# Attention inputs loaded straight into the layout of their transposes, and weight conversions cut into three parts per attention step

## The chip, the cores and the metric

The kernel runs on one core of a Trainium2 chip. The metric is the device time of one execution in microseconds (us). In the profile PE is the matrix engine, PEld its weight loads, DVE the vector engine, ACT the scalar engine, POOL the GpSimd engine and SP the engine that issues most of the transfers. L12 is line 12 of the kernel file.

## The reference

Three computations follow each other; all of the output depends on all three.

```python
# attention: B=4, H=12 heads, S=448, D=64
scores = scale * (q @ k^T) - log(S)
attn_out = sigmoid(scores) @ v                  # -> x, 1792 tokens x 768
# mixture of experts, one expert of 8 per token, F=1024
e = argmax(x @ w_gate);  gate = softmax(x @ w_gate)[e];  eom = sigmoid(x @ w_output_gate)
x[token] = gate * eom[e] * (relu(x @ w1[e]) @ w2[e])
# last stage, d_ff = 2048
h = x @ w_in;  g = h * cos(h);  out = g @ w_out
```

The two matrices of the last stage, `w_in` and `w_out`, arrive as 64-bit floats, and q, k, v and the other weights as 32-bit floats.

## The kernel before

Every matrix product is made of several PE passes over a high and a low part of each operand (`kh`, `kl`; `gh`, `gl`; and so on). ACT rounds a value to its high part, and DVE subtracts that from the value to get the low part.

**Attention** runs from about 0 to 255 us, in 24 steps, one for each batch and pair of heads. A step has two halves, c = 0 and c = 2. In program order, a half does the scores of two of four groups of 112 keys (`sc`, L309; ACT turns them into `aT` with the sigmoid, L312), the transposes of the next step's operands on PE, and the product of the step before with v (`av`, L316). The transposes of c = 0 are those of q (`pq`, L294, then two DVE operations `T`, L302) and of the first head of k (`pk`, L282, then ACT `kh` L286 and DVE `kl` L288); c = 2 has the second head of k, and the transposes of the finished x (`px`, `xr`). The end of a step copies `av` out (`xT`, L326).

The transposes read q as 112 rows of (4 key groups, 2 heads, 64) and k as 112 rows of (4 key groups, the same head twice, 64). Memory holds each head apart. So `load` fetches q, k and v in the order of memory, one transfer each of 1 KB runs, three steps ahead, and `relay` copies two steps ahead: q on POOL (L271), the first head of k on POOL and the second on DVE (L276), the latter two doubling the head.

**Conversions.** The 64-bit weights are turned into two 32-bit parts on chip, in 48 pieces of 128x512 elements, and written back to memory (`wi_d`, `wo_d`) for the last stage. A piece is loaded (`craw`, two buffers); ACT makes `ctu` (L151); DVE makes `cta`, `ctf`, `cta`, `ctf` (L152 to L155); that is the first part of the generator `conv`. The second part is DVE `cta` (L157), ACT `chi` (L159) and three POOL operations (L160, L161, L163), the last of which writes `clo`. `ctu`, `cta` and `ctf` have one buffer each, so a piece's first part waits for the POOL operations of the piece before. An attention step ends with the first part of a piece (`conv_step(False)`), and c = 0 of the next step ends with its second part (`conv_end`). `conv_step` also issues, on SP, the stores of the piece before and the load of the next. Attention does 23 pieces this way; the expert slots bring the count to `CONV_EARLY` = 40; the rest are done in the last stage.

**Experts** run from about 255 to 690 us in slots of 128 tokens, with 17 pieces between them.

**Last stage**, from about 690 us, has 64 units u: 4 blocks of tokens times 16 chunks of d_ff. Iteration u of its loop issues a piece's first part while pieces are left, then `product(u + 1)`, `angle(u + 2)` (five DVE operations, L1152 to L1156, that reduce h for the cosine) and `down(u)` (the product with w_out). `product` multiplies h with its cosine, `r` on DVE (L1167), finishes the pending piece with `conv_end`, and then makes `gh` on ACT (L1171) and `gl` on DVE (L1172). The call `load_w(u + 5)`, ahead of `product`, finishes pieces whole until those are done that its chunk needs. The pieces are done during u = 2 to 9.

The order on each engine is the order in which the program issues; no planner moves it.

Of the kernel before, what the change touches and what calls it, by code (L numbers as in the profile page):

```python
# [9 lines left out]
F32 = mybir.dt.float32  # L10
# [11 lines left out]

GATE_STEPS = 7
NEST = 18
CONV_EARLY = 40
PAUSE = "pause"
NRING = 6
ROUTE_AT = [(0, "relu"), (0, 9), (0, 13), (0, 15), (1, 0), (1, 3), (1, "relu"), (1, 9), (1, 14)]
# [25 lines left out]
def tile_attn_moe_cos(ctx: ExitStack, tc: tile.TileContext, q, k, v, wg, wog, w1, w2, w_in, w_out, out):  # L54
    nc = tc.nc
    B, H, S, D = q.shape
# [4 lines left out]
    CP = 112  # L61
    NC = S // CP
    NPAIR = H // 2
# [40 lines left out]
    first = cst.tile([1, 1], I32, name="first")  # L104
# [24 lines left out]
    def conv_load(i):  # L129
        if i >= len(conv_list):  # L130
            return
        which, h, r = conv_list[i]
        raw = craw[i % 2]
        if which == "i":
            src = w_in[r * P : (r + 1) * P, h * CW : (h + 1) * CW].bitcast(U32)
            nc.sync.dma_start(raw.rearrange("p f t -> p (f t)"), src)
        else:
            src = wo_in[h][:, :, r * CO : (r + 1) * CO].bitcast(U32)
            nc.sync.dma_start(raw.rearrange("p (two f) t -> p two (f t)", two=2), src)

    def conv(i):
        if i >= len(conv_list):
            return
        which, h, r = conv_list[i]
        raw = craw[i % 2]
        low, high = raw[:, :, 0], raw[:, :, 1]
        ta = cta
        tf = conv_p.tile([P, CW], U32, tag="ctf", name="ctf")
        tu = conv_p.tile([P, CW], F32, tag="ctu", name="ctu")
        f = tf.bitcast(F32)  # L150
        nc.scalar.activation(tu, low, AF.Copy, scale=2.0**-52)  # L151
        nc.vector.tensor_scalar(ta, high, 3, 0x3FFFFFF8, op0=ALU.logical_shift_left, op1=ALU.bitwise_and)  # L152
        nc.vector.scalar_tensor_tensor(tf, high, 0xC0000000, ta, op0=ALU.bitwise_and, op1=ALU.bitwise_or)  # L153
        nc.vector.tensor_scalar(ta, high, 0x7FFFFFFF, None, op0=ALU.bitwise_and)
        nc.vector.scalar_tensor_tensor(f, ta.bitcast(F32), LEAST, f, op0=ALU.is_ge, op1=ALU.mult)  # L155
        yield
        nc.vector.tensor_scalar(ta, tf, 0xFF800000, None, op0=ALU.bitwise_and)  # L157
        hi = conv_p.tile([P, CW], F32R, tag="chi", name="chi", bufs=2)
        nc.scalar.activation(hi, f, AF.Copy)  # L159
        nc.gpsimd.tensor_tensor(tu, tu, ta.bitcast(F32), op=ALU.mult)  # L160
        nc.gpsimd.tensor_tensor(f, f, hi.bitcast(F32), op=ALU.subtract)  # L161
        lo = conv_p.tile([P, CW], F32R, tag="clo", name="clo", bufs=2)
        nc.gpsimd.tensor_tensor(lo, tu, f, op=ALU.add)  # L163
        conv_out.append((which, h, r, (hi.bitcast(F32), lo.bitcast(F32))))

    def conv_store():
        while conv_out:
            which, h, r, parts_ = conv_out.pop()
            for t, f in enumerate(parts_):
                if which == "i":  # L170
                    c0 = h * CW // P
                    nc.sync.dma_start(
                        wi_d[c0 : c0 + CW // P, :, t, r, :].rearrange("c p f -> p c f"),
                        f.rearrange("p (c f) -> p c f", f=P),
                    )
                else:
                    nc.sync.dma_start(
                        wo_to[h, t][:, :, r * CO : (r + 1) * CO], f.rearrange("p (two f) -> p two f", two=2)
                    )
# [3 lines left out]
    def conv_step(whole=True):  # L183
        conv_end()
        conv_store()
        conv_load(conv_at[0] + 1)
        conv_rest.append(conv(conv_at[0]))
        next(conv_rest[0], None)
        conv_at[0] += 1
        if whole:  # L190
            conv_end()

    conv_rest = []

    def conv_end():
        while conv_rest:
            next(conv_rest.pop(), None)


    pre = pre_st.enter_context(tc.tile_pool(name="pre", bufs=1, side="right"))  # L200
# [46 lines left out]
    with ExitStack() as st:  # L247
        io = st.enter_context(tc.tile_pool(name="io", bufs=3))
# [3 lines left out]
        ps_sc = ps_s.enter_context(tc.tile_pool(name="ps_sc", bufs=2, side="right", space=PSUM))  # L252
        ps_av = st.enter_context(tc.tile_pool(name="ps_av", bufs=1, space=PSUM))

        srcs = (("q", q), ("k", k), ("v", v))
        vt = [io.tile([CP, 2, NC, D], F32, name=f"v{i}", bufs=1) for i in range(5)]

        def load(b, hp):
            r = {}
            for nm, src in srcs:  # L260
                t = vt[(b * NPAIR + hp) % 5] if nm == "v" else io.tile([CP, 2, NC, D], F32, tag=nm, name=nm, bufs=2)
                nc.sync.dma_start(
                    t.rearrange("p h c d -> p h (c d)"),
                    src[b, 2 * hp : 2 * hp + 2].rearrange("h (p c) d -> p h (c d)", c=NC),
                )
                r[nm] = t
            return r

        def relay(t, first=nc.gpsimd):
            qp = io.tile([CP, NC, 2, D], F32, tag="qp", name="qp", bufs=2)  # L270
            first.tensor_copy(qp.rearrange("p c h d -> p h c d"), t["q"])  # L271
            t["q"] = qp
            for j in range(2):
                kd = io.tile([CP, NC, 2, D], F32, tag=f"kd{j}", name=f"kd{j}", bufs=2)
                eng = nc.vector if j else first
                eng.tensor_copy(kd, t["k"][:, j].unsqueeze(2).to_broadcast([CP, NC, 2, D]))  # L276
                t[f"k{j}"] = kd

        def prep_k(t, j, kk):
            pt = ps_tr.tile([P, 512], F32, tag="tr", name="pk")  # L280
# [212 lines left out]
        items = [(b, hp) for b in range(B) for hp in range(NPAIR)]  # L493
        n = len(items)
        L = {i: load(*items[i]) for i in range(3)}


        relay(L[0], nc.vector)
        wgp = acst.tile([P, KD, 32], F32, name="wgp")
        nc.gpsimd.memset(wgp, 0.0)  # L500
        nc.sync.dma_start(wgp[:, :, 0:E], wg.rearrange("(k p) e -> p k e", p=P))
# [56 lines left out]
        nT0 = prep_q(L[0])  # L558
        prep_k(L[0], 0, kk0)
        prep_k(L[0], 1, kk0)  # L560
        relay(L[1])
        prepd = {0: (kk0, nT0)}
        prev = None
        pend = None
# [12 lines left out]
        for i in range(n):  # L577
            aT = a2.tile([CP, NC, 2, S], F32, tag="aT", name="aT")
            kk, T = prepd.pop(i)
            if prev:  # L580
                pav = ps_av.tile([P, 512], F32, tag="av", name="av")
            if i + 3 < n:
                L[i + 3] = load(*items[i + 3])
            if i == 0:
                conv_load(0)
            elif 6 <= i < 6 + NSLOT - NSURE:
                s = NSURE + i - 6
                nc.sync.dma_start(ys_d[s * P : (s + 1) * P, :], zero)
            if i + 2 < n:
                relay(L[i + 2])  # L590
            if i > 0:
                next(consts, None)
            nk = {}
            nT = None
            for c in range(0, NC, 2):
                scores(c, kk, T, aT)
                scores(c + 1, kk, T, aT)
                if c == 0:
                    if i + 1 < n:
                        nT = prep_q(L[i + 1])  # L600
                        prep_k(L[i + 1], 0, nk)
                else:
                    if pend is not None:
                        tail2(pend)
                        pb, php = items[pend]
                        if pb < B - 1 and php == NPAIR - 1:
                            pg = ps_tr.tile([P, 512], F32, tag="tr", name="pg")
                            gate_mm(pb, range(KD), pg)
                            gates.append(gate(pb, pg))
                        pend = None  # L610
                    if i + 1 < n:
                        prep_k(L[i + 1], 1, nk)
                if prev:
                    av(prev[1], prev[2], c, pav)
                    av(prev[1], prev[2], c + 1, pav)
                if c == 0:
                    conv_end()
                gate_step(GATE_STEPS if i >= n - NPAIR else 1)
                load_step()
                if i == n - 1:  # L620
                    if c == 0:
                        turn(xg0, ps_tr, "tr")
                    else:
                        split(w1r[0], w1h[0], w1l[0], True)
                        nc.sync.dma_start(w2r[0], w2_src_d(e1[0], 0))
            if i + 1 < n:
                prepd[i + 1] = (nk, nT)
            if prev:
                tail1(prev[0], pav)
                pend = prev[0]  # L630
            prev = (i, L.pop(i), aT)
            if i < n - 1:
                conv_step(False)
        assert not gates and not loads
        ps_s.close()
        ps_h = pre_st.enter_context(tc.tile_pool(name="ps_h", bufs=2, side="right", reuse_waits="tile", space=PSUM))
# [67 lines left out]
    with ExitStack() as st:  # L704
# [54 lines left out]
        def slot(s, between, when):  # L759
# [4 lines left out]
            with when():  # L764
# [50 lines left out]
                if s == 0:  # L815
                    split2(2)
                    split2(3)
            if s >= 1 and conv_at[0] < CONV_EARLY:
                conv_step()
# [224 lines left out]
        def last_slots(s):  # L1044
            assert conv_at[0] >= CONV_EARLY
            act = nc.values_load(fl[0:1, 2, s : s + 1], min_val=0, max_val=1)
# [27 lines left out]
    with ExitStack() as st:  # L1074
# [175 lines left out]
        for u in range(N):  # L1250
            bi, c = units[u]
# [51 lines left out]
```

## Time and profile before

| | |
|---|---|
| median of 3 runs | 1198.21 us (1194.3, 1198.21, 1198.25) |
| the profiled execution's own time | 1196.37 us |
| its span, first to last instruction | 1194.7 us |
| mean granted PE clock | 0.977 of full speed |
| busy: PE, DVE, ACT, POOL | 91%, 65%, 43%, 33% of the span |

The span is 1.7 us shorter than the execution. The busy shares are means over the three stages; in attention DVE is busier than in the whole, and in the expert slots less.

### The profile page before, as it was taken

How to read it: one execution, taken by the hardware profiler on the slowest of the kernel's cores; microseconds unless marked ns; L12 is line 12 of the kernel's file. 1: busy time of each engine (PE TensorE's matmuls, PEld its weight loads, DVE VectorE, ACT ScalarE, POOL GpSimd, SP SyncE). 2: the span in 40 equal slices, each digit the busy share in tenths (PEclk: the TensorE clock that was granted, in tenths of full speed). 3: DMA queues.
4: the chain of work that ended last, by engine and by line, in shares of the span. 5: the costliest groups of instructions: out<-in, count | busy, mean ns of one | idle time of the engine just before them, and what ended most of it. 6: DMA issues, size and time to landing. Idle time of an engine off the chain costs nothing. (4 is left out here: it accounts for less than half of the span.)

```text
span 1194.7 us, 17366 instructions
## 1 busy us (share of the span) xinstructions
PE 1089.3 (91%) x5740; PEld 870.0 (73%) x5740; DVE 778.7 (65%) x1239; ACT 509.0 (43%) x754; POOL 393.5 (33%) x306
## 2 busy tenths in 40 slices
PE   7899999888998899789789789979999999999997
PEld 5555555546777688568568568858888889999996
DVE  5878887967655844774774648996555555566553
ACT  6666666643242513442542433334323333333332
POOL 4665555372144532663651603440200002001001
PEclk9999999998998999899999989989999999999999
DMA  6778776463538562885784487747665558767751
GB/s 173 197 225 237 222 197 198 143 220 108 209 106 275 182 205 91 268 290 165 254 289 154 134 343 282 270 181 294 217 246 183 188 187 328 264 222 292 262 190 41
DMA packets 118795, 254.72 MB, mean 213 GB/s; under 512 B 9440, under 2 KB 66016, under 8 KB 118688
## 3 DMA queue, kind: packets, MB, share of 16 engines
q1 hardware_dynamic: 114768, 234.19, 57.8%
q0 software_dynamic: 3920, 19.28, 5.0%
q8 instruction: 47, 0.77, 0.3%
q14 instruction: 60, 0.49, 0.1%
HBM read 207.02 MB, written 46.41 MB: 212 GB/s over the span
## 5 line engine op out<-in xcount | busy, mean ns | idle before, releaser
L160 POOL TENSOR_TENSOR ctu<-ctu,cta 128x512 f32<-128x512 f32 x48 | 62.0, 1291 | 325.5 <-DVE cta L157 244.5
L1198 PE MATMUL o<-wo,gh 128*128 128x512 f32 x448 | 168.4, 397 | 0.0
L1222 POOL DMA_INDIRECT out_dram<-osb,at x14 | 14.2, 1011 | 358.8 <-DVE osb L1211 267.5
L1138 PE MATMUL ph<-yh,wi 128*128 128x512 f32 (+1 forms) x318 | 116.3, 366 | 8.2 <-ACT p L1147 5.3
L243 PE MATMUL p<-w1l,xh 128*128 128x512 f32 x228 | 95.1, 417 | 30.5 <-DVE w1l L218 27.9
L1161 ACT ACTIVATE r<-r 128x512 f32<-128x512 f32 (+1 forms) x64 | 37.0, 578 | 188.2 <-DVE r L1156 186.6
L1139 PE MATMUL ph<-yl,wi 128*128 128x512 f32 (+1 forms) x318 | 115.9, 364 | 0.0
L1140 PE MATMUL ph<-yh,wi 128*128 128x512 f32 (+1 forms) x318 | 115.8, 364 | 0.0
L1199 PE MATMUL or<-wo,gh 128*128 128x256 f32 x384 | 108.3, 282 | 0.0
L242 PE MATMUL p<-w1h,xh 128*128 128x512 f32 x228 | 95.7, 420 | 4.9 <-ACTq L755 2.7
L1198 PEld LDWEIGHTS o<-wo,gh 128*128 128x128 f32 x448 | 84.1, 188 | 17.5 <-ACT gh L1171 0.4
L312 ACT ACTIVATE aT<-sc,b_sig 112x896 f32<-112x896 f32 x96 | 91.4, 1004 | 6.7 <-PE sc L309 6.4
L244 PE MATMUL p<-w1h,xl 128*128 128x512 f32 x228 | 92.9, 407 | 0.0
L1198 PE MATMUL o<-wo,gl 128*128 128x512 f32 x224 | 88.4, 395 | 0.7 <-DVE gl L1172 0.7
L316 PE MATMUL av<-aT,v 112*64 112x448 f32 x384 | 84.5, 563 | 0.0
L1167 DVE TENSOR_TENSOR r<-r,p 128x512 f32<-128x512 f32 (+1 forms) x64 | 39.9, 624 | 66.0 <-ACT r L1162 66.0
L309 PE MATMUL sc<-T,kl 128*112 128x448 f32 x192 | 73.1, 381 | 9.9 <-DVE kl L288 9.8
L218 DVE TENSOR_TENSOR w1l<-rw,w1h 128x1536 fp32r<-128x1536 f32 x22 | 72.3, 3336 | 14.0 <-ACT w1h L217 8.8
L243 PEld LDWEIGHTS p<-w1l,xh 128*128 128x128 f32 x228 | 45.1, 198 | 46.4 <-DVE w1l L218 35.7
L309 PE MATMUL sc<-T,kh 128*112 128x448 f32 x192 | 75.7, 394 | 2.3 <-ACT kh L286 1.6
L1152 DVE TENSOR_SCALAR t<-p 128x512 f32<-128x512 f32 (+1 forms) x64 | 33.8, 528 | 65.8 <-ACT p L1147 65.8
L731 ACT ACTIVATE hh<-pht 128x512 fp32r<-128x512 f32 x38 | 22.6, 595 | 119.0 <-PE pht L728 119.0
(259 smaller groups left out, 2807.7 us busy)
## 6 DMA issues: line engine op xcount, KB each, us to landing
rw<-in_moe_w_dram SPq DMA_DIRECT2D x64, 768.0 KB, 6.0
wo<-wo_d SPq DMA_DIRECT2D x64, 768.0 KB, 4.5
wi<-wi_d SPq DMA_DIRECT2D x53, 768.0 KB, 5.9
craw<-in_moe_w_in_dram SPq DMA_DIRECT2D x25, 512.0 KB, 5.3
craw<-in_moe_w_out_dram SPq DMA_DIRECT2D x24, 512.0 KB, 4.8
er<-wi_d SPq DMA_DIRECT2D x11, 768.0 KB, 6.6
ys_d<-ysb SPq DMA_DIRECT2D x19, 384.5 KB, 3.8
wi_d<-chi SPq DMA_DIRECT2D x24, 256.0 KB, 3.3
```

Source lines behind the costliest of these rows:

```text
L218: (nc.gpsimd if pool else nc.vector).tensor_tensor(lo, raw, hi.bitcast(F32), op=ALU.subtract)
L242: nc.tensor.matmul(ps, xh[:, kc], wh, start=first, stop=False)
L243: nc.tensor.matmul(ps, xh[:, kc], wl, start=False, stop=False)
L244: nc.tensor.matmul(ps, xl[:, kc], wh, start=False, stop=last)
L309: nc.tensor.matmul(ps[:, j, :S], kk[j][part][:, c * CP : (c + 1) * CP], T[j], start=s, stop=not s)
L312: nc.scalar.activation(aT[:, c], ps[:, :, :S], AF.Sigmoid, bias=b_sig[:CP], scale=1.0 / math.sqrt(D))
L316: nc.tensor.matmul(pav[D * j : D * j + D, :S], t["v"][:, j, c, :], aT[:, c, j], start=c == 0, stop=c == NC - 1)
L1138: nc.tensor.matmul(ph[:, :w], wih[:, kc], yh[:, kc, :w], start=kc == 0, stop=False)
L1139: nc.tensor.matmul(ph[:, :w], wih[:, kc], yl[:, kc, :w], start=False, stop=False)
L1140: nc.tensor.matmul(ph[:, :w], wil[:, kc], yh[:, kc, :w], start=False, stop=kc == KD - 1)
L1198: nc.tensor.matmul(acc[i], g[:, ts_], w[:, :512], start=f, stop=l)
L1199: nc.tensor.matmul(acc["r", i], g[:, ts_], w[:, 512:], start=f and (own or i % 2 == 0), stop=l, skip_group_check=True,)
```

## The change

`relay` and its copies go. `load` fetches q with two transfers and k with four, each head of k twice, into the layouts that the transposes read; the runs in memory are now 256 bytes. The q and k tiles keep two buffers each, and the transposes read them directly. `conv` gets a second `yield`, so it has three parts: ACT `ctu` and DVE `cta`, `ctf`; then DVE `cta`, `ctf`; then the old second part. In attention steps 1 to 22 the first part ends c = 0, the second ends c = 2, and the third stands at the end of the step, behind the copy `xT`. In the last stage `conv_step(False)` issues only the first part ahead of `product`, and `conv_end` the two others behind the multiplication `r`.

```diff
-CONV_EARLY = 40
+CONV_EARLY = 39
...
         nc.vector.scalar_tensor_tensor(tf, high, 0xC0000000, ta, op0=ALU.bitwise_and, op1=ALU.bitwise_or)
+        yield
         nc.vector.tensor_scalar(ta, high, 0x7FFFFFFF, None, op0=ALU.bitwise_and)
...
-        next(conv_rest[0], None)
+        conv_next()
...
+    def conv_next():
+        if conv_rest and next(conv_rest[0], conv_rest) is conv_rest:
+            conv_rest.pop()
+
     def conv_end():
         while conv_rest:
-            next(conv_rest.pop(), None)
+            conv_next()
...
-            for nm, src in srcs:
-                t = vt[(b * NPAIR + hp) % 5] if nm == "v" else io.tile([CP, 2, NC, D], F32, tag=nm, name=nm, bufs=2)
-                nc.sync.dma_start(
-                    t.rearrange("p h c d -> p h (c d)"),
-                    src[b, 2 * hp : 2 * hp + 2].rearrange("h (p c) d -> p h (c d)", c=NC),
-                )
-                r[nm] = t
+            two = slice(2 * hp, 2 * hp + 2)
+            r["q"] = io.tile([CP, NC, 2, D], F32, tag="q", name="q", bufs=2)
+            for j in range(2):
+                nc.sync.dma_start(r["q"][:, :, j], q[b, 2 * hp + j].rearrange("(p c) d -> p c d", c=NC))
+            for j in range(2):
+                r[f"k{j}"] = io.tile([CP, NC, 2, D], F32, tag=f"k{j}", name=f"k{j}", bufs=2)
+                for h in range(2):
+                    nc.sync.dma_start(r[f"k{j}"][:, :, h], k[b, 2 * hp + j].rearrange("(p c) d -> p c d", c=NC))
...
-        def relay(t, first=nc.gpsimd):
-            qp = io.tile([CP, NC, 2, D], F32, tag="qp", name="qp", bufs=2)
-            first.tensor_copy(qp.rearrange("p c h d -> p h c d"), t["q"])
-            t["q"] = qp
-            for j in range(2):
-                kd = io.tile([CP, NC, 2, D], F32, tag=f"kd{j}", name=f"kd{j}", bufs=2)
-                eng = nc.vector if j else first
-                eng.tensor_copy(kd, t["k"][:, j].unsqueeze(2).to_broadcast([CP, NC, 2, D]))
-                t[f"k{j}"] = kd
...
-            if i + 2 < n:
-                relay(L[i + 2])
...
-                if c == 0:
-                    conv_end()
+                if c == 0 and 0 < i < n - 1:
+                    conv_step(False)
+                elif c > 0:
+                    conv_next()
...
-            if i < n - 1:
-                conv_step(False)
+            conv_end()
```

On DVE in an early attention step, the kernel before issues, from the copy of k to the next piece's first part:

```order
L276 COPY kd_394<-k 112x512
L302 TENSOR_TENSOR T_414<-pq,T_414 64x448
L302 TENSOR_TENSOR T_415<-pq,T_415 64x448
L288 TENSOR_TENSOR kl_427<-pk,kh_425 128x448
L157 TENSOR_SCALAR cta<-ctf 128x512
L337 COPY xr<-px 112x4x128
L288 TENSOR_TENSOR kl_466<-pk,kh_464 128x448
L326 COPY xT<-av 128x448
L152 TENSOR_SCALAR cta<-craw_100 128x512
L153 SCALAR_TENSOR_TENSOR ctf<-craw_100,cta 128x512
L154 TENSOR_SCALAR cta<-craw_100 128x512
L155 SCALAR_TENSOR_TENSOR ctf<-cta,ctf 128x512
```

The changed kernel has there, on DVE:

```order
L303 TENSOR_TENSOR T_404<-pq,T_404 64x448
L303 TENSOR_TENSOR T_405<-pq,T_405 64x448
L289 TENSOR_TENSOR kl_417<-pk,kh_415 128x448
L152 TENSOR_SCALAR cta<-craw_101 128x512
L153 SCALAR_TENSOR_TENSOR ctf<-craw_101,cta 128x512
L338 COPY xr<-px 112x4x128
L289 TENSOR_TENSOR kl_457<-pk,kh_455 128x448
L155 TENSOR_SCALAR cta<-craw_101 128x512
L156 SCALAR_TENSOR_TENSOR ctf<-cta,ctf 128x512
L327 COPY xT<-av 128x448
L158 TENSOR_SCALAR cta<-ctf 128x512
```

The copy of k is gone, two operations of the piece stand behind the first `kl`, two behind the second, and the last at the step's end, so that the POOL operations which it releases now begin there.

On SP, one attention step before issues three loads, two stores of a piece and the load of another:

```order
L262 DMA q<-in_q_dram 112x2x256
L262 DMA k<-in_k_dram 112x2x256
L262 DMA v_126<-in_v_dram 112x2x256
L172 DMA wi_d<-chi 128x4x128
L172 DMA wi_d<-clo 128x4x128
L136 DMA craw_100<-in_moe_w_in_dram 128x1024
```

and in the changed kernel:

```order
L269 DMA q<-in_q_dram 112x4x64 x2
L273 DMA k_576<-in_k_dram 112x4x64 x2
L273 DMA k_579<-in_k_dram 112x4x64 x2
L275 DMA v_127<-in_v_dram 112x2x256
L173 DMA wi_d<-chi 128x4x128
L173 DMA wi_d<-clo 128x4x128
L136 DMA craw_100<-in_moe_w_in_dram 128x1024
```

Ten issues stand where six stood, six of them in runs of 64 elements.

In the last stage, at u = 9, where pieces run out, DVE before goes from the transposed tokens' low part `yl` through one piece to `r` and `gl`:

```order
L1127 TENSOR_TENSOR yl<-pyt,yh 128x512
L152 TENSOR_SCALAR cta<-craw_101 128x512
L153 SCALAR_TENSOR_TENSOR ctf<-craw_101,cta 128x512
L154 TENSOR_SCALAR cta<-craw_101 128x512
L155 SCALAR_TENSOR_TENSOR ctf<-cta,ctf 128x512
L157 TENSOR_SCALAR cta<-ctf 128x512
L1167 TENSOR_TENSOR r<-r,p 128x512
L1172 TENSOR_TENSOR gl<-r,gh 128x512
```

and in the changed kernel:

```order
L1125 TENSOR_TENSOR yl<-pyt,yh 128x512
L152 TENSOR_SCALAR cta<-craw_100 128x512
L153 SCALAR_TENSOR_TENSOR ctf<-craw_100,cta 128x512
L155 TENSOR_SCALAR cta<-craw_100 128x512
L156 SCALAR_TENSOR_TENSOR ctf<-cta,ctf 128x512
L158 TENSOR_SCALAR cta<-ctf 128x512
L152 TENSOR_SCALAR cta<-craw_101 128x512
L153 SCALAR_TENSOR_TENSOR ctf<-craw_101,cta 128x512
L155 TENSOR_SCALAR cta<-craw_101 128x512
L156 SCALAR_TENSOR_TENSOR ctf<-cta,ctf 128x512
L158 TENSOR_SCALAR cta<-ctf 128x512
L1165 TENSOR_TENSOR r<-r,p 128x512
L1170 TENSOR_TENSOR gl<-r,gh 128x512
```

Attention has 22 pieces instead of 23 and the expert slots 17 as before, so one more is left, and `load_w(14)` at u = 9 asks for it behind that iteration's own: two whole pieces stand ahead of `r`.

## Rows read from the trace of the kernel before

**Rows 1.** Windows: start:end, length, five engines' busy us, PEclk, DMA share, GB/s.

```profile
24.00:204.00 180.00, 164.80 (x910) 97.37 (x908) 145.62 (x236) 121.11 (x181) 104.91 (x100) 1.00 0.74 209
767.00:807.00 40.00, 31.50 (x145) 24.79 (x143) 37.09 (x51) 14.45 (x25) 17.92 (x13) 0.91 0.55 200
```

**Rows 2.** Chain that ended last, 795:815: start, length, what.

```profile
807.53 0.61 DVE yl L1127
808.18 0.66 PE pyt L1123 x4
```

**Rows 3.** Waits, 24:205: engine, line <- releaser: total us, times, longest.

```profile
ACT ctu L151 <- POOL clo L163: 42.4, 18, 2.4
...
PE pk L282 <- DVE T L302: 10.2, 13, 0.9
```

**Rows 4.** Timeline, one attention step: start, length, instruction, [idle before <- releaser].

```profile
112.88 1.90 ACT L312 ACTIVATE aT<-sc,b_sig 112x896 f32<-112x896 f32 x2
113.13 0.42 DVE L157 TENSOR_SCALAR cta<-ctf 128x512 uint32<-128x512 uint32 x1
...
113.69 1.27 POOL L160 TENSOR_TENSOR ctu<-ctu,cta 128x512 f32<-128x512 f32 x1 [4.36 <-DVE m L372]
...
114.66 0.55 ACT L286 ACTIVATE kh<-pk 128x448 fp32r<-128x448 f32 x1
...
115.25 0.63 DVE L288 TENSOR_TENSOR kl<-pk,kh 128x448 fp32r<-128x448 f32 x1 [1.01 <-ACT kh L286]
...
115.79 0.46 DVE L374 TENSOR_TENSOR oh<-eq,m 112x32 bf16<-112x32 f32 x1
...
117.60 0.70 ACT L151 ACTIVATE ctu<-craw 128x512 f32<-128x512 uint32 x1 [2.39 <-POOL clo L163]
...
118.18 1.01 ACT L312 ACTIVATE aT<-sc,b_sig 112x896 f32<-112x896 f32 x1
```

**Rows 5.** Timeline of the first steps, before POOL converts.

```profile
18.76 0.43 DVE L154 TENSOR_SCALAR cta<-craw 128x512 uint32<-128x512 uint32 x1
19.22 0.69 DVE L155 SCALAR_TENSOR_TENSOR ctf<-cta,ctf 128x512 f32<-128x512 f32 x1
19.83 0.42 DVE L276 COPY kd<-k 112x512 f32<-112x512 f32 x1
...
28.07 1.90 ACT L312 ACTIVATE aT<-sc,b_sig 112x896 f32<-112x896 f32 x2
```

**Rows 6.** Timeline, starts of the last attention steps.

```profile
208.34 1.89 ACT L312 ACTIVATE aT<-sc,b_sig 112x896 f32<-112x896 f32 x2
...
244.58 1.93 ACT L312 ACTIVATE aT<-sc,b_sig 112x896 f32<-112x896 f32 x2 [1.36 <-PE sc L309]
```

**Rows 7.** Waits in the last attention steps, 205:262.

```profile
PE sc L309 <- DVE kl L288: 7.1, 3, 2.4
```

**Rows 8.** Timeline of the last stage, a middle unit and u = 9.

```profile
745.88 0.72 ACT L1162 ACTIVATE r<-r,b_half 128x512 f32<-128x512 f32 x1
746.35 0.43 DVE L154 TENSOR_SCALAR cta<-craw 128x512 uint32<-128x512 uint32 x1
...
797.85 0.69 DVE L153 SCALAR_TENSOR_TENSOR ctf<-craw,cta 128x512 uint32<-128x512 uint32 x1
...
799.76 0.43 DVE L157 TENSOR_SCALAR cta<-ctf 128x512 uint32<-128x512 uint32 x1
800.11 0.68 DVE L1167 TENSOR_TENSOR r<-r,p 128x512 f32<-128x512 f32 x1
```

**Rows 9.** Transfers, 28.5:29.1: queue, packets, MB, share of 16 engines.

```profile
q1 hardware_dynamic: 340, 0.17, 93.4%
```

**Rows 10.** Transfers, 9.8:10.6: packets by size, then the queue.

```profile
DMA packets 864, 0.09 MB, mean 113 GB/s; under 512 B 800, under 2 KB 864, under 8 KB 864
...
q1 hardware_dynamic: 864, 0.09, 89.5%
```

**Rows 11.** Transfers, whole run: target, queue, kind, count, KB each, landing.

```profile
craw<-in_moe_w_in_dram SPq DMA_DIRECT2D x25, 512.0 KB, 5.3
```

More of the change, by code (lines that the diff above doesn't have):

```diff
@@ L253, in tile_attn_moe_cos @@
         ps_av = st.enter_context(tc.tile_pool(name="ps_av", bufs=1, space=PSUM))
-        srcs = (("q", q), ("k", k), ("v", v))
         vt = [io.tile([CP, 2, NC, D], F32, name=f"v{i}", bufs=1) for i in range(5)]
@@ L259, in load @@
             r = {}
-            for nm, src in srcs:
-                t = vt[(b * NPAIR + hp) % 5] if nm == "v" else io.tile([CP, 2, NC, D], F32, tag=nm, name=nm, bufs=2)
-                nc.sync.dma_start(
-                    t.rearrange("p h c d -> p h (c d)"),
-                    src[b, 2 * hp : 2 * hp + 2].rearrange("h (p c) d -> p h (c d)", c=NC),
-                )
-                r[nm] = t
-            return r
-        def relay(t, first=nc.gpsimd):
-            qp = io.tile([CP, NC, 2, D], F32, tag="qp", name="qp", bufs=2)
-            first.tensor_copy(qp.rearrange("p c h d -> p h c d"), t["q"])
-            t["q"] = qp
-            for j in range(2):
-                kd = io.tile([CP, NC, 2, D], F32, tag=f"kd{j}", name=f"kd{j}", bufs=2)
-                eng = nc.vector if j else first
-                eng.tensor_copy(kd, t["k"][:, j].unsqueeze(2).to_broadcast([CP, NC, 2, D]))
-                t[f"k{j}"] = kd
+            two = slice(2 * hp, 2 * hp + 2)
[6 more added lines that the diff above has]
+                    nc.sync.dma_start(r[f"k{j}"][:, :, h], k[b, 2 * hp + j].rearrange("(p c) d -> p c d", c=NC))
+            r["v"] = vt[(b * NPAIR + hp) % 5]
+            nc.sync.dma_start(
+                r["v"].rearrange("p h c d -> p h (c d)"), v[b, two].rearrange("h (p c) d -> p h (c d)", c=NC)
+            )
+            return r
         def prep_k(t, j, kk):
@@ L495, in tile_attn_moe_cos @@
         L = {i: load(*items[i]) for i in range(3)}
-        relay(L[0], nc.vector)
         wgp = acst.tile([P, KD, 32], F32, name="wgp")
@@ L560, in tile_attn_moe_cos @@
         prep_k(L[0], 1, kk0)
-        relay(L[1])
         prepd = {0: (kk0, nT0)}
```

## The prediction

> **What bounds the kernel now.** The windows come first, because the three stages have different limits [rows 1]. In attention PE is busy 164.80 of 180 us, or 9.16 of each 10.0 us step, DVE 81% and the transfer engines 74%: no engine is full, so a loop of waits must set the step. The waits name it [rows 3]: ACT stands 18 times, 2.4 us each, in front of `ctu` until POOL has written `clo`, while PE loses only 10.2 us to its commonest wait there. The timeline gives the loop [rows 4]: DVE `cta` (L157) at 113.13 releases three POOL operations, which end where `ctu` starts, at 117.60; `aT` follows on ACT at 118.18, with the next step's scores, transposes and first part behind it. Eighteen steps from 28.07 [rows 5] to 208.34 [rows 6] make 180.27 us, 10.015 each.
>
> In the last stage the reading is the other way round. From 767 to 807 us DVE is busy 37.09 of 40 us, PE 31.50 [rows 1]. The chain of waits runs through DVE until `yl` releases PE at 808.18 [rows 2], and from there on PE's own products carry it. What delays DVE before 808 delays the end.
>
> **The change part by part.** *The loop in attention.* The copies disappear and POOL is released at the end of the step. I follow the new loop with rows of before. Head 1 of k: `kh` to `kl` 0.59 (114.66 to 115.25); `kl` to the next DVE operation 0.54 (to 115.79) [rows 4]. `cta` to `ctf` 0.46, `ctf` to the next 0.61 before POOL converts [rows 5]. Then the copy `xT`, as long as `kl`, 0.54; `cta` to POOL 0.56 (113.13 to 113.69); POOL to `ctu` 3.91 (113.69 to 117.60); `ctu` to `aT` 0.58; `aT` to `kh` of head 1 1.78 (112.88 to 114.66) [rows 4]. The sum is 9.57 us against 10.015: 0.445 less per step, 8.0 us in 18 steps. PE's 9.16 still fits inside. Small gate operations of the expert choice stand in c = 2 between `kl` and `xT`: I put 0.15 us of them into each step, 2.7 us in all; at the 0.46 of `oh` beside POOL [rows 4] they would take the whole 8.0, at nothing none. I take 5.3, with ends 0 and 8.
>
> *The ends of attention.* The last steps take 36.24 us for three (208.34 to 244.58) [rows 6], 6.2 more than three of 10.015, and there PE waits 7.1 us for `kl` in three waits [rows 7]: DVE does many gate operations beside POOL. With POOL released only at the end of the step, c = 2 runs without it. I take back half of the 6.2, 3 us (ends 0 and 6). The copies before the first step and the piece that attention no longer holds give 1.5 (0 to 3). What is late next is PE, for `kl` of head 1. Attention: 5.3 + 3 + 1.5 = 9.8 us, called 10; by the ends 0 to 17, and since three terms do not all end on one side, 4 to 13.
>
> *The transfers.* q and k took 448 KB in 1 KB runs; k is now read twice, so there are 672 KB in 2688 packets of 256 bytes a step. No row has this size. From 28.5 to 29.1 us, 340 packets of 512 bytes took 0.6 x 16 x 0.934 / 340 = 26.4 ns each [rows 9]. From 9.8 to 10.6, 800 of 864 packets are 32-byte ones of the gate weights (0.09 MB in all), and with the whole time put to them they took 0.8 x 16 x 0.895 / 800 = 14.3 ns [rows 10]. Linearly between 32 and 512 bytes, 256 costs 20 ns: 2688 x 20 / 16 engines = 3.4 us, against 896 x 26.4 / 16 = 1.5 before. The transfer engines' 7.4 us per step become 9.3 of 9.57. At the upper end, 26.4 ns, the loads take 4.4 and the step 10.3; at the lower, 14.3 ns, 2.4 and 8.3. I cost the transfers at nothing, because the loads are three steps ahead; the cover is thin. The new wait is SP's. With two buffers a load overwrites the tile that this very step transposes; head 1 of k is transposed just before its `kh`, which stands 6.5 us into the step (114.66 less 118.18 - 10.01) [rows 4]. Behind that wait SP still has v, two stores and the load of the next piece, so `craw` is issued some 8 us into the step (an estimate), lands 5.3 later [rows 11], at 3.7 of the next, and is read behind `kl` of head 0, about 5 us in: 1 us of slack. Each microsecond beyond it would cost up to 22, one for each piece.
>
> The rows on packet cost leave a gap that the Trainium skill fills against this change: "DMA: Bandwidth & Descriptors", section "Specifications", gives 512 bytes as the least transfer for line rate and says that below it the engines read, modify and write. The 32-byte loads at no more than 14.3 ns do not look like a doubled access [rows 10], so the sum goes without it. If it did apply, as twice the time of half a 512-byte packet, each would cost 26.4 ns, the upper end above.
>
> *The last stage, order.* In u = 2 to 8 `r` stood behind the first four DVE operations of a piece; now it stands behind two. ACT gives the cosine at 745.88 + 0.72 = 746.60, and DVE would come to it at 746.35 [rows 8], so it waits 0.3; then `cta`, `ctf` follow `r` by 0.61, and `chi`, `gh` and `gl` stand behind them: `gl` comes about 0.95 later. POOL starts only 0.3 later, so of the DVE operations behind `gl`, slowed beside POOL, fewer fall under it; that returns about half. With the ends 0 and 0.95 I take 0.35 for six units: 2 us (0 to 6).
>
> *The last stage, one more piece.* One piece moves from attention to u = 9, where two whole pieces now stand ahead of `r`. The second's `ctf` must wait until POOL has written the first's `clo`. Before, `cta` started at 799.76 and `r` at 800.11 [rows 8]. After: 799.76 + 0.56 + 3.88 for POOL (the 3.91 less the semaphore) = 804.20, and from `ctf` to `r` 2.26 (797.85 to 800.11) [rows 8] gives 806.46: 6.3 us later, and `yl` to PE with it. The lower end is 2.3, the second piece's own operations, were POOL done.
>
> *Sum.* In the profiled execution's own time: 1196.4 - 10 + 2 + 6.3 = 1194.7 us. The median of the runs is 1.8 above that execution, the lowest 2.1 below. I predict 1196.
>
> **The rivals.** *The loss in the last stage is not paid* (faster). PE could absorb the 6.3 where its queue is behind anyway. For it: PE is at 79% to 808 us, so it has slack somewhere; against it: `yl` releases PE directly, and PE's order is fixed. With 2 of the 8.3 paid: 1196.4 - 10 + 2 = 1188.4; called 1189.
>
> *The transfers become the bound* (slower). The place is attention; the price is 2688 packets a step; it decides from about 22 ns a packet, where the 7.4 - 1.5 us that remain and the loads fill 9.57. At 26.4 ns a step is 10.3 us: 18 x (10.3 - 10.015) = 5.1 us slower, the ends gain nothing, and with the last stage's 8.3 the sum is 1209.8, called 1210. At 35 ns, a third more than the 512-byte row, a step is 11.8, and the sum 1237. For it: 74% busy now, 1 us of slack for `craw`, and a size that no row shows; against it: the 32-byte row.
>
> *Attention gains little* (within). The loop closes elsewhere: on DVE a piece's first part now stands between `kl` of head 0 and `xr`, which PE's next transposes wait for. For it: 0.445 us a step is the small difference of sums of nine terms, and an error of 0.02 in each halves it. With 3 gained: 1196.4 - 3 + 8.3 = 1201.7.
>
> **How the numbers follow.** The forecast, 1196 with its own range 1191 to 1201, has 0.40; the unpaid loss 0.23; the transfers 0.20; the small gain 0.17. Half a per cent, 6 us, is what a measurement can tell from no change: the bounds are 1192.2 and 1204.2. Faster: 0.10 of the forecast and 0.20 of the unpaid loss, 0.30. Slower: 0.19 of the transfers and 0.06 of the small gain, 0.25. The rest, 0.45, is within. The range, 1186 to 1213, leaves out the upper part of the transfers' case and of the attention gain.
>
> **What would show it.** Right: steps of 9.6 to 9.8 us in the middle of attention, PE's wait there on `kl` instead of `T`, no copies on POOL, and a transfer share of 0.9; last-stage units some 0.35 us longer; at u = 9 a DVE wait for `clo` of about 4 us. Wrong: a transfer share at 0.95 or more with steps above 10.015 (the transfers); steps of 9.9 with the wait still on `clo` (small gain); a wait of PE on `yl` after u = 9 no longer than before (unpaid loss). It would be wrong altogether if ACT or SP came to wait for q, k or `craw` in the middle of attention.

## The result and the profile after

The changed kernel took 1211.2 us (median of 4 runs, 1210.18 to 1214.49) against 1196.26 for the kernel before (4 runs): a ratio of 1.0131, 95% interval 1.0098 to 1.0164. It is slower. The forecast was 1196, no change; 1211 lies inside the range, at the price of the transfers' rival.

The profiled execution took 1210.48 us, with a span of 1208.8, 14.1 more than before. Starts of instructions cut the two spans into the same pieces: the first sigmoid `aT` of attention steps 2, 20 and 23 [rows 5, 6], and the `gh` of units 2 and 10 of the last stage. The two `gh` of before, and the rows of after, ACT:

```profile
720.29 0.63 ACT L1171 ACTIVATE gh<-r 128x512 fp32r<-128x512 f32 x1 [0.76 <-DVE r L1167]
...
800.82 0.63 ACT L1171 ACTIVATE gh<-r 128x512 fp32r<-128x512 f32 x1 [0.42 <-DVE r L1167]
```

```profile
31.67 1.89 ACT L313 ACTIVATE aT<-sc,b_sig 112x896 f32<-112x896 f32 x2
...
216.49 1.89 ACT L313 ACTIVATE aT<-sc,b_sig 112x896 f32<-112x896 f32 x2
...
249.58 1.89 ACT L313 ACTIVATE aT<-sc,b_sig 112x896 f32<-112x896 f32 x2
...
725.60 0.63 ACT L1169 ACTIVATE gh<-r 128x512 fp32r<-128x512 f32 x1 [0.76 <-DVE r L1165]
...
814.95 0.63 ACT L1169 ACTIVATE gh<-r 128x512 fp32r<-128x512 f32 x1 [0.43 <-DVE r L1165]
```

| us | before | after | difference | forecast |
|---|---|---|---|---|
| to step 2 | 28.07 | 31.67 | +3.6 | -1.5 |
| 18 steps | 180.27 | 184.82 | +4.55 | -5.3 |
| last three steps | 36.24 | 33.09 | -3.15 | -3 |
| experts, to unit 2 | 475.71 | 476.02 | +0.3 | 0 |
| units 2 to 10 | 80.53 | 89.35 | +8.8 | +8.3 |
| rest | 393.9 | 393.9 | 0 | 0 |

Two of the six rows miss, both in attention. The window of attention after, in the columns of [rows 1]:

```profile
24.00:204.00 180.00, 163.87 (x869) 94.16 (x867) 107.42 (x209) 118.95 (x174) 69.23 (x60) 0.99 0.81 222
```

DVE fell from 145.62 to 107.42 us in attention and POOL from 104.91 to 69.23, and still the steps are longer: work off the bound was removed. The transfers' share is 0.81, so they are not full. The waits of ACT and DVE, 24 to 205 us, as in [rows 3]:

```profile
ACT ctu L151 <- DMA craw<-in_moe_w_in_dram: 10.7, 7, 3.5
...
ACT ctu L151 <- DMA craw<-in_moe_w_out_dram: 7.3, 5, 1.8
ACT ctu L151 <- POOL clo L164: 1.6, 6, 0.3
```

The 42.4 us for `clo` of before are 1.6 now; in their place stand 18.0 us on 12 late pieces. And SP's own queue there waits for the transposes (`pk`) before it may load over them:

```profile
SPq L273 <- PE pk L283: 28.3, 14, 3.9
SPq L269 <- PE pk L283: 22.6, 13, 5.0
```

The late step that begins at 153.70, with the step ahead of it, which begins at 144.13 and in which its piece is loaded, in the timeline of SP, PE, POOL and ACT:

```profile
144.13 1.89 ACT L313 ACTIVATE aT<-sc,b_sig 112x896 f32<-112x896 f32 x2
...
145.53 6.44 SPq L273 DMA_DIRECT2D k<-in_k_dram  x4
...
148.45 0.69 ACT L151 ACTIVATE ctu<-craw 128x512 f32<-128x512 uint32 x1 [0.21 <-POOL clo L164]
...
150.10 0.60 PE L283 MATMUL pk<-ident,k 112*128 112x112 f32 x4
...
152.02 0.60 SPq L275 DMA_DIRECT2D v<-in_v_dram  x1
152.72 0.40 SPq L178 DMA_DIRECT2D wo_d<-chi  x1
153.22 0.41 SPq L178 DMA_DIRECT2D wo_d<-clo  x1
...
153.70 1.89 ACT L313 ACTIVATE aT<-sc,b_sig 112x896 f32<-112x896 f32 x2
153.73 2.20 SPq L136 DMA_DIRECT2D craw<-in_moe_w_in_dram  x1
...
157.20 1.29 POOL L164 TENSOR_TENSOR clo<-ctu,ctf 128x512 fp32r<-128x512 f32 x1
...
160.18 0.69 ACT L151 ACTIVATE ctu<-craw 128x512 f32<-128x512 uint32 x1 [2.38 <-DMA craw<-in_moe_w_in_dram]
...
160.77 1.88 ACT L313 ACTIVATE aT<-sc,b_sig 112x896 f32<-112x896 f32 x2
```

SP starts the four loads of k at 145.53 and is held until `pk` has run (from 150.10); v and two stores follow; `craw` goes out at 153.73 and is there when `ctu` starts, at 160.18. POOL's `clo` was done at 158.5 (157.20 + 1.29), so the loop stood still for 1.7 us, and `aT` behind it. Where the piece is on time the loop is as worked out: steps 2 and 3 take 9.57 and 9.61.

### The profile page after: what moved, and what is told of

Read it like the earlier page. It is cut to its first block, busy times and chain, and to the rows that moved or that the text cites. A ratio compares the mean times of both kernels' runs of the same rounds, so it can differ in the third digit from the quotient of the medians.

```text
span 1208.8 us, 17442 instructions
## 1 busy us (share of the span) xinstructions
PE 1100.5 (91%) x5740; PEld 874.8 (72%) x5740; DVE 733.6 (61%) x1213; ACT 510.2 (42%) x754; POOL 356.6 (29%) x260
## 5 line engine op out<-in xcount | busy, mean ns | idle before, releaser
L248 PE MATMUL p<-w1l,xh 128*128 128x512 f32 x228 | 96.5, 423 | 29.1 <-DVE w1l L223 26.7
L1220 POOL DMA_INDIRECT out_dram<-osb,at x14 | 14.2, 1011 | 358.8 <-DVE osb L1209 267.5
L160 ACT ACTIVATE chi<-ctf 128x512 fp32r<-128x512 f32 x48 | 30.4, 633 | 105.8 <-DVE ctf L156 56.4
L310 PEld LDWEIGHTS sc<-T,kh 128*112 128x112 f32 x192 | 34.5, 180 | 53.9 <-ACT aT L313 30.7
```

The lines of the kernel that those rows point to most:

```text
L248: nc.tensor.matmul(ps, xh[:, kc], wl, start=False, stop=False)
L310: nc.tensor.matmul(ps[:, j, :S], kk[j][part][:, c * CP : (c + 1) * CP], T[j], start=s, stop=not s)
```

## The experiments

Theory A: the loss in attention is lateness by order on SP, where the piece's load stands behind loads that wait for this step's transposes. Theory B: the 256-byte packets fill the transfer engines. Theory C: the ten issues are by themselves too slow.

**A third buffer** for the tiles of q and k.

```diff
-            r["q"] = io.tile([CP, NC, 2, D], F32, tag="q", name="q", bufs=2)
+            r["q"] = io.tile([CP, NC, 2, D], F32, tag="q", name="q", bufs=3)
...
-                r[f"k{j}"] = io.tile([CP, NC, 2, D], F32, tag=f"k{j}", name=f"k{j}", bufs=2)
+                r[f"k{j}"] = io.tile([CP, NC, 2, D], F32, tag=f"k{j}", name=f"k{j}", bufs=3)
```

> The q and k tiles get three buffers instead of two, all else as in the changed kernel. Theory A (order on SP): in attention the loop itself is 9.57 us, and the steps are longer only where the next piece arrives late, because SP stands at the loads of q and k until this step's transposes have read the old tiles, with the piece's load behind them. With a third buffer SP has no such wait: steps 2 to 20 return to 9.6 to 9.8 us, the last step's first sigmoid from 249.6 to about 239, time about 1200. Theory B (packets of 256 bytes fill the transfer engines): the number of packets is the same, so steps stay at 10.2 or more and the time within 3 us of 1211. Theory C (the ten issues on SP by themselves take too long): in between, half of the gain.

Measured: 1199.38 us, ratio to the kernel before 1.0012 (0.9997 to 1.0028). The 18 steps take 173.84 us, 9.658 each. Its window:

```profile
24.00:204.00 180.00, 173.72 (x940) 100.44 (x939) 114.36 (x224) 126.02 (x185) 73.03 (x63) 1.00 0.96 242
```

The same packets, now at a share of 0.96, and steps of 9.66: theory B falls, and so does theory C by itself, since the issues are as many as before. Of SP's 50.9 us of waits for `pk` at the loads of q and k, 3.1 are left, the largest part being

```profile
SPq L273 <- PE pk L283: 2.7, 4, 1.3
```

One late piece is left, at the start (2.3 us).

**The piece's load first**, on two buffers.

```diff
+            if i < n - 1:
+                conv_load(i)
             if i + 3 < n:
                 L[i + 3] = load(*items[i + 3])
-            if i == 0:
-                conv_load(0)
-            elif 6 <= i < 6 + NSLOT - NSURE:
+            if 6 <= i < 6 + NSLOT - NSURE:
```

> The load of the next piece is issued ahead of the step's seven loads instead of behind them; buffers, packets and the number of issues as in the changed kernel. Theory A, and theory C as well: the piece is there 8 us or more before its use, ACT and DVE never wait for it, steps 2 to 20 are 9.6 to 9.8 us, the second step loses its 3 us too, time about 1196 to 1199. Theory B: no change of more than 3 us, and the wait moves to q, k or the piece again.

Measured: 1196.13 us, ratio 0.9989 (0.997 to 1.0008); 18 steps in 173.82 us, the time to step 2 28.11. ACT's only wait for a piece's input is the short one for `clo`, and SP still waits, harmlessly:

```profile
ACT ctu L151 <- POOL clo L164: 5.6, 18, 0.7
```

```profile
SPq L274 <- PE pk L284: 20.3, 13, 3.2
```

Moving one issue ahead of seven returns, by the trace, 11.0 us in the 18 steps and 3.6 ahead of them. SP's 20.3 us of waits cost nothing once no urgent load stands behind them. Theories A and C both expected this; it is the third buffer that tells them apart.

**Long runs**: the same bytes in the same seven transfers, 1 KB at a time; q and k then stand in the wrong order in their tiles.

```diff
-                nc.sync.dma_start(r["q"][:, :, j], q[b, 2 * hp + j].rearrange("(p c) d -> p c d", c=NC))
+                nc.sync.dma_start(
+                    r["q"].rearrange("p c h d -> p (c h d)")[:, 256 * j : 256 * j + 256],
+                    q[b, 2 * hp + j].rearrange("(p c) d -> p (c d)", c=NC),
+                )
...
```

> The same seven transfers of the same bytes into the same tiles in the same order, but in runs of 1 KB, so that q and k stand in the wrong order in their tiles and the values, with them the choice of experts, are others: only the attention stage is read. Theory A: a late piece stays late, steps mean 10.0 to 10.3 us, SP still waits for the transposes. Theory B: with a quarter of the packets the steps fall to 9.6 to 9.8 us. Theory C: the time of an issue decides; if a 1 KB run is issued faster (0.41 us in the kernel before against 0.62 to 0.66), a good part of the loss goes too.

Measured, attention alone: 18 steps in 180.46 us, 10.025 each, with 8.5 us of ACT's waits for late pieces; step 2 begins at 26.13, against 31.67 in the changed kernel. So the run length has a share. The first issues on SP in this kernel:

```profile
0.82 0.87 SPq L269 DMA_DIRECT2D q<-in_q_dram  x2
1.73 1.84 SPq L276 DMA_DIRECT2D k<-in_k_dram  x4
3.61 0.43 SPq L281 DMA_DIRECT2D v<-in_v_dram  x1
...
15.82 0.46 SPq L136 DMA_DIRECT2D craw<-in_moe_w_in_dram  x1
```

and the changed kernel's:

```profile
0.82 1.40 SPq L269 DMA_DIRECT2D q<-in_q_dram  x2
2.26 2.61 SPq L273 DMA_DIRECT2D k<-in_k_dram  x4
4.92 0.61 SPq L275 DMA_DIRECT2D v<-in_v_dram  x1
...
20.72 0.46 SPq L136 DMA_DIRECT2D craw<-in_moe_w_in_dram  x1
```

A load of q or k in 1 KB runs is issued in 0.45 us, in 256-byte runs in 0.65 to 0.7, and v behind them, whose runs are 1 KB in both, in 0.43 and 0.61. Over seven loads that is some 1.4 us a step, and the first piece goes out 5 us later. Of the 0.61 us a step that the changed kernel loses (10.267 less 9.658), 0.37 stays with long runs, and 0.24 goes with the short ones: by SP's longer issues (theory C) or by the packets themselves, which this run doesn't tell apart. The 0.24 is rough, since it compares one execution with one: the run with the old order in the last stage, below, has the attention of the changed kernel, and its steps take 10.434.

**Old loads** and copies, with all that is done to the conversions.

```diff
-            r["q"] = io.tile([CP, NC, 2, D], F32, tag="q", name="q", bufs=2)
...
+            for nm, src in srcs:
+                t = vt[(b * NPAIR + hp) % 5] if nm == "v" else io.tile([CP, 2, NC, D], F32, tag=nm, name=nm, bufs=2)
...
+            if i + 2 < n:
+                relay(L[i + 2])
```

> The loads and copies of the kernel before with all that the change does to the conversions (three parts, 22 pieces in attention, the last stage's order and its extra piece). All theories that put the loss on the loads: no late piece, steps 2 to 20 at 9.6 to 9.9 us (the copies on POOL fit beside its 3.9 us, the one on DVE adds up to 0.4), attention 5 to 10 us shorter than before, the last stage 8.8 longer, time 1195 to 1201. If the loss were in the new order of the parts, attention would stay at the changed kernel's length, about 1210.

Measured: 1197.77 us, ratio 1.0 (0.9987 to 1.0013); 18 steps in 175.08 us, 9.727 each. The three parts alone carry nearly the whole gain in attention; the loads bring 0.07 us a step where the piece is on time.

**Old order in the last stage**, on the changed kernel.

```diff
                 conv_step(False)
+                conv_next()
```

> The changed kernel, with the second part of a piece put ahead of the multiplication r in the last stage again; the extra piece at u = 9 stays. Read from the start of the third to that of the eleventh gh (units 2 to 10), which takes 80.5 us before and 89.35 in the changed kernel. If the order costs 0.4 us a unit and the extra piece 6 us, as the sum had it: 86.5. If the order costs nothing, 89.3; if it costs all, 80.5.

Measured: units 2 to 10 in 86.84 us; the order costs 2.5, the rest 6.3 is the extra piece. Its one time, 1214.05, says nothing of that: its 18 steps in attention, the same code as in the changed kernel, take 187.81 us, 3.0 more than there. The wait at u = 9 in this kernel, DVE:

```profile
810.35 0.43 DVE L158 TENSOR_SCALAR cta<-ctf 128x512 uint32<-128x512 uint32 x1
812.25 1.48 DVE L152 TENSOR_SCALAR cta<-craw 128x512 uint32<-128x512 uint32 x1 [1.47 <-POOL ctu L161]
814.89 0.69 DVE L153 SCALAR_TENSOR_TENSOR ctf<-craw,cta 128x512 uint32<-128x512 uint32 x1 [1.15 <-POOL clo L164]
```

From the first piece's `cta` to the second's `ctf` it is 4.54 us; 4.44 was forecast. But it is not one wait of 4 us for `clo`, as the prediction's sign had it: DVE waits 1.47 us for `ctu` and 1.15 for `clo`, with a `cta` of 1.48 between.

**A 23rd piece in the last attention step**, on the kernel with the piece first, in place of the extra one at u = 9.

```diff
-CONV_EARLY = 39
+CONV_EARLY = 40
...
-                if c == 0 and 0 < i < n - 1:
+                if c == 0 and i > 0:
```

> The kernel with the piece's load ahead of the seven, and a 23rd piece in the last attention step, so that the last stage has eight again, one for each u from 2 to 9; its order as in the changed kernel. Units 2 to 10 of the last stage: 83 us if the two pieces at u = 9 cost 6, 89 if they cost nothing. The last attention step has a piece more: 0 to 3 us longer.

Measured: units 2 to 10 in 83.43 us, 5.9 less than 89.33. But the first hidden values of the experts, `hh`, come 32.04 us after the last step's first `aT`, against 24.65 without the piece: 7 us are lost where 0 to 3 were expected. (The kernel before, which has 23 pieces, has them at 28.04.) Its one time is 1195.27.

**Both together**, the piece first.

> Both together on the kernel with the piece's load ahead of the seven: the 23rd piece in attention and the old order in the last stage. Units 2 to 10: 80.5 us as before. With attention some 9 us shorter than before and nothing lost behind it, the time is 1186 to 1190, faster than the kernel before by 0.6 to 0.9%.

Measured: units 2 to 10 in 80.55 us, as before the change; attention 9.5 us shorter; the time 1194.37 us, ratio 0.997 (0.9953 to 0.9987). A gain of 0.3%, where 0.6 to 0.9% was expected: `hh` is at 31.75 us again.

**The same with old loads.**

> The loads and copies of the kernel before, with the three parts in attention, the 23rd piece there and the old order in the last stage. It tells what the direct loads are worth once the piece is on time: by the 9.73 us steps that old loads had with three parts, against 9.66 with direct loads and the piece first, 1.3 us in 18 steps and 1 to 2 at the start: 1188 to 1192. If the copies cost more than that, 1193 or above.

Measured: 1194.81 us, ratio 0.9969 (0.9953 to 0.9986), where 1188 to 1192 was expected: the direct loads make no difference here. The 23rd piece costs some 5 us with old loads (`hh` at 32.72, against 27.47 with 22 pieces).

**Nine pieces from u = 1**, on the kernel with the piece first and the old order, with 22 pieces in attention.

```diff
-            if u > 1 and conv_at[0] < len(conv_list):
+            if u > 0 and conv_at[0] < len(conv_list):
```

> The piece's load ahead of the seven, 22 pieces in attention, the old order in the last stage, and its nine pieces begun at u = 1 instead of u = 2, so that none stands twice. The first product behind the last attention step then does not have the 23rd piece before it, which had cost 4 to 5 us there. Price: one more unit of 10.3 us in place of 7.2 or less, 3 to 4 us, against 5.9 for the two at u = 9. Attention 9.5 us shorter than before, last stage 3 to 4 longer: 1190 to 1194, faster than before by 0.3 to 0.6%. If the expert slots give back what attention gains whatever is done, no change from before.

Measured: 1189.52 us, ratio 0.9943 (0.992 to 0.9966). `hh` comes at 24.74 us, and units 2 to 10 take 83.58. It beats both kernels. The last step and `hh` there, ACT:

```profile
238.48 1.91 ACT L314 ACTIVATE aT<-sc,b_sig 112x896 f32<-112x896 f32 x2
259.24 0.60 ACT L730 ACTIVATE hh<-pht 128x512 fp32r<-128x512 f32 x1 [8.09 <-PE pht L727]
```

and in the kernel with both, the piece first and 23 pieces:

```profile
241.97 1.91 ACT L314 ACTIVATE aT<-sc,b_sig 112x896 f32<-112x896 f32 x2
...
268.01 0.60 ACT L729 ACTIVATE hh<-pht 128x512 fp32r<-128x512 f32 x1 [13.35 <-PE pht L726]
```

ACT waits 5 us longer for it, and it is 8.8 us later. 3.5 of them are there at this `aT`. Then POOL does the piece's three operations among those that prepare the first expert's weights (from 248.75 to 252.57), and a later low part, `w2l`, falls beside DVE's `oh` of the expert choice, which PE waits for. `oh` takes 3.12 us there, and 0.19 behind POOL in the kernel with 22 pieces, here below:

```profile
259.43 3.42 POOL L224 TENSOR_TENSOR w2l<-rw,w2h 128x1536 fp32r<-128x1536 f32 x1
259.77 3.12 DVE L376 TENSOR_TENSOR oh<-eq,m 112x32 bf16<-112x32 f32 x1
262.94 0.25 PE L849 MATMUL pp<-oh,ones 112*128 112x8 bf16 x4 [4.71 <-DVE oh L376]
```

```profile
255.85 0.19 DVE L376 TENSOR_TENSOR oh<-eq,m 112x32 bf16<-112x32 f32 x1
256.10 0.24 PE L850 MATMUL pp<-oh,ones 112*128 112x8 bf16 x4 [1.95 <-DVE oh L376]
```

PE's wait is 2.8 us longer by it. The 2.5 us that are left of the 8.8 are not followed here.

**And that with old loads.**

> The same with the loads and copies of the kernel before. If direct loads are worth as little as the steps say (9.73 against 9.66 us), the same time as the run with direct loads within 0.2%; if removing the copies has a worth of its own, 3 us or more above it.

Measured: 1193.22 us, ratio 0.9971 (0.9955 to 0.9986). That is 3.7 us above the run with direct loads, beyond the 3 that the expectation set for a worth of their own, and by the trace attention (from the first `aT` to the last step's) is 223.56 us with them and 226.36 without, 2.8 less. The pair with 23 pieces showed 0.4 us of it. So the direct loads are worth 0 to some 3 us, and how much stays open.

## Why the prediction was wrong

The sum failed in one step: "I cost the transfers at nothing, because the loads are three steps ahead". The same paragraph had the mechanism, SP's wait for this step's transposes with the load of `craw` behind it, and its price of up to 22 us for each microsecond; but it took an estimated 1 us of slack as cover, and ACT met a late piece 12 times in some 18 steps. ACT did come to wait for `craw` in the middle of attention, the prediction's own sign of being wrong altogether. The sizes of the estimate were short. The transpose was on time: SP's wait in the step that begins at 144.13 ends 6.6 us in, where 6.5 stood.

```profile
150.74 1.23 SPq L273 DMA_DIRECT2D k<-in_k_dram  x2
```

But the two held loads of k themselves, 1.23 us, were left out of what follows the wait, and v takes 0.60 behind short runs. So `craw` is issued 9.6 us in, where 8 stood, and it needs 6.4 us to land, not 5.3 [rows 11]; 2.2 of these are its own issue on SP, for which the first piece needed 0.46. That is 2.7 us against some 1 of slack, and 1.7 us of wait. In a step on time the slack is smaller still: ACT's `ctu` reads the piece 4.3 us in (148.45 less 144.13), ahead of DVE's read, which the estimate took at about 5. Over the 18 pieces loaded in steps 2 to 19 the issue comes 7.9 to 10.6 us into its step, 8.6 in the median, and the landing takes 5.1 to 7.0, 6.2 in the median. The medians of all landings from 24 to 205 us, before and after:

```profile
craw<-in_moe_w_in_dram SPq DMA_DIRECT2D x10, 512.0 KB, 5.3
craw<-in_moe_w_out_dram SPq DMA_DIRECT2D x8, 512.0 KB, 4.6
```

```profile
craw<-in_moe_w_in_dram SPq DMA_DIRECT2D x11, 512.0 KB, 5.6
craw<-in_moe_w_out_dram SPq DMA_DIRECT2D x7, 512.0 KB, 6.3
```

What it cost is the difference to the kernel with the piece first: 18 steps 184.82 less 173.82, 11.0 us, and 3.6 to step 2. Added to the forecast's 1194.7 that makes 1209.3; the profiled execution has 1210.5.

Of the other terms one gave nothing and the rest held. *The start*, 1.5 us for the copies before the first step and the piece less: with the piece first, step 2 begins at 28.11, against 28.07 before. *The loop*: 9.57 us without a wait, as summed from nine rows; with the piece first 9.657 in the mean, gate operations included, a gain of 6.4 in 18 steps where 5.3 stood. *The last three steps*: -3.15 for -3, and PE's 7.1 us of waits for `kl` there [rows 7] are 1.1. *The order in the last stage*: 2.5 for 2. *The extra piece*: 5.9 to 6.3 for 6.3; the rival in which this is not paid is refuted, since `yl` releases PE 96.0 us behind the `gh` of unit 2, against 87.2 before [rows 2], and nothing of the 8.8 comes back behind unit 10:

```profile
821.61 0.61 DVE yl L1125
822.27 0.66 PE pyt L1121 x4
```

*The rival that named the transfers as the bound* came out at 1210, but by luck and for another reason than its own: it asked for steps of 10.3 us at a share of 0.95, and what came was steps between 9.57 and 11.72 at 0.81, 10.27 in the mean, with 12 named waits for late pieces; with the order mended the same packets run at 0.96 and steps of 9.66. *The packets*: from 33.5 to 38 us only 256-byte ones were moving,

```profile
DMA packets 1700, 0.42 MB, mean 93 GB/s; under 512 B 1700, under 2 KB 1700, under 8 KB 1700
...
q1 hardware_dynamic: 1700, 0.42, 41.2%
```

4.5 x 16 x 0.412 / 1700 = 17.5 ns each, for 20 in the sum and 26.4 for twice that size [rows 9]. The two were taken at different shares, 41% and 93%, so their ratio is rough. By the Trainium skill, "DMA: Bandwidth & Descriptors", section "Why small descriptors are slow (HBM only)", a 256-byte packet is 8 beats and 3 cycles of overhead, 11 in all; 512 bytes would then be 19 (an estimate), a ratio of 0.58. The trace has 0.66, nearer to that than to the ratio of 1 that the prediction took for the read-modify-write below 512 bytes. That one stands in the section "Specifications" of the same page of the Trainium skill, and no run shows it.

*Attention gains little* is refuted too: with the piece on time, from the first `aT` to the last step's, it takes 17.3 + 173.8 + 33.4 = 224.6 us against 18.0 + 180.3 + 36.2 = 234.5 before, 9.9 less; from the span's start it is 9.2, since the first `aT` comes 0.7 later.

What stays open: whether the 0.24 us a step that go with long runs are SP's issue time or the packets; and why executions of one kernel spread by several us. The expert stage, from the last attention step to unit 2, is 484.3 us in the profile with a third buffer, the slowest of that kernel's ten executions, and 470.1 in that with the piece first, the fastest of its ten. The windows of the two:

```profile
236.74:721.01 484.27, 421.03 (x2109) 341.12 (x2110) 290.38 (x399) 180.63 (x227) 202.52 (x106) 0.95 0.60 203
235.35:705.44 470.09, 409.14 (x2112) 330.66 (x2111) 290.23 (x399) 180.83 (x226) 203.46 (x106) 0.97 0.61 207
```

PE is busy 11.9 us longer in the first, at a granted clock of 0.95 instead of 0.97, and DVE as long in both: most of the 14.2 us goes with the clock. Why the clock differs is not shown. The kernel from u = 1 took 1183.68 us at a granted clock of 0.983 over the span, and 1193.48 at 0.970.

## What to carry to other kernels

Before a transfer is made to write a buffer that is still being read, list what stands behind it on its queue, and issue ahead of it whatever has a due time: one issue moved gave back all that the new wait had cost. Slack of a microsecond that rests on an estimated issue time is no cover; cost it as a wait with a chance, and count the held loads themselves among what follows the wait. And a piece of background work is cheap only where its engines have room: one more conversion cost 6 us where two stood together at u = 9, 5 to 7 at the border of two stages, and 3 to 4 as a unit more at u = 1.

## What the runs showed of the hardware

The busy share of the transfer engines is not a fixed amount of work: the same packets read as 0.81 x 10.27 = 8.3 us a step in the changed kernel and 0.96 x 9.66 = 9.3 with a third buffer, where only one late piece was waited for. SP's time to issue a load of q or k at the kernel's start grew from 0.45 us with runs of 1 KB to 0.65 with runs of 256 bytes, and that of the unchanged load of v behind them from 0.43 to 0.61. One issue of `craw` took 2.20 us on SP in a late step, against 0.46 at the start.
